# Strassen's seven products for the first FFN product, with the sums of w1's quarters kept in DRAM

## The chip, the cores and the metric

The kernel runs on one core of one Trainium2 chip. Times are device microseconds of one execution. Before the change the median of three runs is 784.04 us (782.01 to 784.25).

## The reference

Four batches of 768 tokens pass through attention with 8 heads of 64 channels (4 sink keys and a window of 128), then a Fourier mix, and then an FFN with a normalization in front:

```python
X = np.fft.fft(np.fft.fft(x, axis=1), axis=2)
u = x + np.real(X).astype(np.float32)
mu = np.mean(u, axis=-1, keepdims=True)
var = np.mean((u - mu) ** 2, axis=-1, keepdims=True)
un = (u - mu) / np.sqrt(var + 1e-06)
ch = np.maximum(un @ w_ch1, 0.0) @ w_ch2
return (u + ch).astype(np.float32)
```

`w_ch1` is 512 x 2048 and `w_ch2` is 2048 x 512. Their entries come as 64-bit floats.

## The kernel before, in words

The work has two stages. The first (to about 225 us of the span) is attention and the Fourier mix, one batch after another. The second is the FFN. Only the second is touched.

The 24 blocks of 128 tokens are cut into **groups** of 4, 2, 4, 4, 4, 4 and 2 blocks (L262). The 2048 hidden features are cut into 16 **feature blocks** f of 128. For one group and one f:

- `ch1` (L612) makes the first product: the weights are w1's block f, the moving operand is the normalized tokens, turned so that channels lie on partitions. Each operand is split into a high and a low part, and a product is high x high, high x low and low x high. So there are 4 channel chunks x 3 = 12 matmuls (L620), of 512 columns for a group of four blocks and of 256 for a group of two, into one PSUM bank.
- `relu` (L1119, ScalarE) makes the high part h of the ReLU, and `relu_lo` (L1124, VectorE) the low part.
- `ch2` (L1126) makes the second product: the weights are now h (128 tokens each), the moving operand is w2's block f of 512 columns; 3 matmuls per token block (L1131), accumulated over all f in one bank per token block.

After the last f, `finish` adds the residual (L1135, VectorE) and stores the block (L1136, SyncE's queue).

**Order.** In group 0 the Tile scheduler orders the work. While this group runs, all 32 weight blocks are loaded in turn (`load_w`, L577; w1's and w2's alternate) and converted (`convert`, L585): three VectorE passes (L591 to L593) make a 32-bit float of a 64-bit one, ScalarE takes the high part (L608), GpSimd the low part (L609). What is left of the last batch's Fourier mix runs beside it. All split weights then stay in SBUF. `prepare(1)` normalizes group 1.

Groups 1 to 6 stand under `tc.manual_schedule()` (L1244): each engine runs its instructions in the order in which the code issues them. For each f the code issues `ch1(f)`, the two ReLU steps, and then `advance`, which issues `ch2` of the f before. A product is thus always one block of twelve matmuls ahead of the use of its ReLU. Behind that come three steps of `prepare` for the next group: statistics, normalization (L539), the turn of a block by VectorE's 32 x 32 transposes (L1155), and the split of the turned block (L549 on ScalarE, L554 on VectorE).

PSUM has eight banks: four for the second product's sums, two ("h") for `ch1`, and one each of "fft" and "n", which serve the Fourier mix and the turns.

```python
def advance(item):
    nonlocal prev
    if prev is not None:
        g, f, h, po = prev
        ch2(f, h, po)
        if f == NF - 1:
            finish(g, po, state[g][0])
    prev = item
```

Of the kernel before, what the change touches and what calls it, by code (L numbers as in the profile page):

```python
# [13 lines left out]
I32 = mybir.dt.int32  # L14
# [32 lines left out]
W_FOLD = 12  # L47
NWA, PER_F, PREP = 14, 2, 11
# [3 lines left out]
CONV_AT, CH1_AT = (3, 5, 7, 9), (9, 10)  # L52
# [3 lines left out]
PREP_AT, PREP_M = 1, 3  # L56
RELOAD_AT = 1
# [149 lines left out]
def kernel(  # L207
# [28 lines left out]


# [24 lines left out]
    sizes = [4, 2, 4, 4, 4, 4, 2]  # L262
# [8 lines left out]
    def run(general):  # L271
        tag = "g" if general else ""
        with ExitStack() as p1:
# [302 lines left out]

            def load_w(i):  # L577
                if i < 2 * NF:
                    f, which = divmod(i, 2)
# [5 lines left out]
            def convert(i, pool=None):  # L585

                r = raw.pop(i)
                t = npool.tile([P, 512], I32, tag="qs0", name=f"cv{i}", bufs=QSB)

                w = t if pool is None or i < NWA else ps_fft.tile([P, 512], I32, tag="fft", name=f"cw{i}", bufs=1)  # L590
# [5 lines left out]
                if i < 4:  # L596

                    if i == 0:
                        state["ring"] = npool.tile([P, 8, 512], F32R, tag="ring", name="w_ring", bufs=1)
                    d = [state["ring"][:, 2 * i + j] for j in range(2)]  # L600
                elif W_FOLD <= i < W_FOLD + NHALF:

                    if i == W_FOLD:
                        state["fold"] = [npool.tile([P, NHALF, DM], F32R, tag=t, name=f"w_{t}", bufs=1) for t in ("gh", "gl")]
                    d = [t[:, i - W_FOLD] for t in state["fold"]]
                else:
                    d = [pool.tile([P, 512], F32R, name=f"w{i}_{j}") for j in range(2)]
                A.copy(d[0], tf)  # L608
                G.tensor_tensor(d[1], tf, f32(d[0]), op=ALU.subtract)  # L609
                Wt[divmod(i, 2)] = d  # L610

            def ch1(g, f, unT):  # L612
# [4 lines left out]
                for cc in range(NCC):  # L617
                    cs = slice(P * cc, P * cc + P)
                    for a, x in ((w[0], unT[0]), (w[0], unT[1]), (w[1], unT[0])):
                        T.matmul(ps[:, :tb], a[:, cs], x[:, :, cc, :], start=n == 0, stop=n == 3 * NCC - 1)  # L620
# [3 lines left out]
            def start_ffn(s):  # L624
# [4 lines left out]
                for i in range(4):  # L629
                    at(s + CONV_AT[i], "V", lambda i=i: convert(i))  # L630
# [477 lines left out]
            def relu(g, f, ps):  # L1108
                tb = P * len(groups[g])
                if g == 0 and un_last:  # L1110

                    t = un_last[0][:, 1].rearrange("p i c t -> p (i c t)")
                    h = [t[:, 1024 * (f % 2) + 512 * i:1024 * (f % 2) + 512 * i + 512] for i in range(2)]
                elif g == 0:
                    h = [g0.tile([P, tb], F32R, tag=f"h{i}", name=f"h{i}_{g}_{f}", bufs=2) for i in range(2)]
                else:
                    h = npool.tile([P, 2, tb], F32R, tag="ld", name=f"h_{g}_{f}", bufs=LDB)
                    h = [h[:, 0], h[:, 1]]
                A.activation(h[0], ps[:, :tb], AF.Relu)  # L1119
                return h  # L1120

            def relu_lo(g, ps, h):
                tb = P * len(groups[g])
                V.scalar_tensor_tensor(h[1], ps[:, :tb], 0.0, f32(h[0]), op0=ALU.max, op1=ALU.subtract)  # L1124
# [8 lines left out]
            def finish(g, po, us):  # L1133
                for i, (b, blk) in enumerate(groups[g]):
                    V.tensor_tensor(us[i], po[i], us[i], op=ALU.add)  # L1135
                    nc.sync.dma_start(out[b, blk], us[i])  # L1136
# [14 lines left out]
            def turn_blocks(un, unf, a):  # L1151

                r = slice(32 * a, 32 * a + 32)
                for q in range(4):
                    V.transpose(unf[32 * q:32 * q + 32, :, r],  # L1155
                                un[r].rearrange("p (c q j) -> p c q j", c=NCC, q=4)[:, :, q])

            def prepare(g):

                us = [u_of(b, blk) for b, blk in groups[g]]  # L1160
                slot = un_slots if g % 2 == 0 else un_last[0]
                unT = [slot[:, :len(us) // 2, i] for i in range(2)]
                state[g] = us, unT
# [7 lines left out]
                for i, u in enumerate(us):  # L1171
# [3 lines left out]
                    if g <= 2:  # L1175

                        pool, tag = banks[1 if g == 1 else i % 2][:2]
                        un_turn(b, blk, pool.tile([P, 512], F32, tag=tag, name=f"unt_{g}_{i}", bufs=1))
                        yield
                    else:  # L1180
                        unf = npool.tile([P, NCC, P], F32, tag="qs0", name=f"unf_{g}_{i}", bufs=QSB)
                        un = un_.pop((b, blk))
                        for a in range(4):
                            turn_blocks(un, unf, a)
                            yield
                        un_[b, blk] = unf.rearrange("p c t -> p (c t)")
                    un_hi(b, blk, unT, i)
                    un_lo(b, blk, unT, i)
                    yield


            pw = None
            un_last = []
            with (tc.manual_schedule() if MAN0 else ExitStack()):
                def do(n):
                    nonlocal s
                    for _ in range(n):
                        for e in ENGINES:
                            run_ev(s, e)
                        s += 1  # L1200

                us = [uview(b)[blk] for b, blk in groups[0]]
                po = [ps_o.tile([P, DM], F32, tag=f"o{i}", name=f"o{i}_0") for i in range(len(us))]
                hs = {}
                for f in range(NF):
                    ps = hp.pop(0) if f < 2 else ch1(0, f, unT0)
                    if f == PREP:
                        ch2(f - 1, hs.pop(f - 1), po)
                        pg.close()
                        wl = p1.enter_context(tc.tile_pool(name="wl" + tag, bufs=1))  # L1210
                        un_last.append(wl.tile([P, 2, 2, NCC, 2 * P], F32R, name="un_last"))
                    hs[f] = relu(0, f, ps)
                    relu_lo(0, ps, hs[f])
                    if pw is None:
                        do(PER_F)
                    if f > 0 and f != PREP:
                        ch2(f - 1, hs.pop(f - 1), po)
                    for i in range(2 * f + 4, min(2 * f + 6, 2 * NF)):
                        if i >= NWA and pw is None:
                            while ev:  # L1220
                                do(1)
                            pf.close()
                            pw = p1.enter_context(tc.tile_pool(name="wb" + tag, bufs=1))
                        convert(i, wa if pw is None else pw)
                    if f == PREP:
                        steps = prepare(1)
                    for _ in range(PREP_N if f >= PREP else 0):
                        next(steps, None)
# [115 lines left out]
```

## Time and profile before

| what | value |
|---|---|
| median of three runs | 784.04 us |
| profiled execution, first to last instruction | 781.4 us |
| median less that span | 2.6 us |
| mean granted TensorE clock | 0.996 |
| matmuls of the first FFN product, L620, largest two groups | 576 and 432 |
| matmuls of the second FFN product, L1131, largest group | 876 |
| mean DMA rate over the span | 74 GB/s |

The span is all that the profile shows of an execution; the 2.6 us lie around it. In the rows below, PE is TensorE's matmuls, PEld its weight loads, DVE VectorE, ACT ScalarE, POOL GpSimd, and SPq the DMA queue of SyncE. A row of the timeline has the start and the length in us, the engine, the line, the operation, output <- input, the shape and the count of merged instructions; in brackets stands how long the engine was idle before and what released it. The length of several merged matmuls runs to the modelled end of the last, which overlaps the next ones, so that the pace is read from starts. A row of groups has, behind the bar, the busy time in us and the mean of one in ns, and behind the next bar the idle time before them.

### The profile page before, as it was taken

The numbers are of one execution on the slowest core, as the hardware profiler recorded it, in microseconds if no ns is written. First come the engines' busy times: TensorE is split into PE (matmuls) and PEld (weight loads), VectorE is DVE, ScalarE is ACT, GpSimd is POOL, SyncE is SP. The second block draws the span as 40 slices with busy tenths as digits, with TensorE's granted clock in tenths as the row PEclk, the third lists the DMA queues.
The fourth block names the chain that finished last, engine by engine and source line by source line (L and its number), as shares of the span: only waits on it lengthen the run. The fifth ranks groups of instructions, "written<-read, shape, count | busy, mean of one in ns | idle before, by whom it ended". The sixth has DMA issues, their size and how long they took to land.

```text
span 781.4 us, 11894 instructions
## 1 busy us (share of the span) xinstructions
PE 755.7 (97%) x4379; PEld 617.1 (79%) x4379; DVE 452.4 (58%) x1318; ACT 237.4 (30%) x704; POOL 183.2 (23%) x295
## 2 busy tenths in 40 slices
PE   8999999989998999999999999999999999999996
PEld 6676876867777878899888888888888888888895
DVE  6878587998999589561456424661456424611211
ACT  4787766766533133221111101111111111110110
POOL 2567477577664245100000000000000000000000
PEclk9999999999999999999999999999999999999999
DMA  9763535434214266110100002000200001000100
GB/s 307 250 176 106 146 83 185 120 118 142 84 54 162 96 206 211 56 55 1 55 0 1 1 37 71 1 0 1 81 0 1 1 8 47 1 0 1 55 1 31
DMA packets 41810, 57.67 MB, mean 74 GB/s; under 512 B 2796, under 2 KB 27500, under 8 KB 41360
## 3 DMA queue, kind: packets, MB, share of 16 engines
q1 hardware_dynamic: 41456, 53.07, 21.7%
q0 software_dynamic: 288, 3.76, 1.2%
q8 instruction: 36, 0.59, 0.3%
q14 instruction: 30, 0.25, 0.1%
HBM read 47.37 MB, written 9.45 MB: 73 GB/s over the span
## 4 chain that ended last, share of the span: by engine, by line
PE 81%; DVE 10%; POOL 4%; issue 2%; ACT 2%; DMA 0%; SPq 0%; ACTq 0%; DVEq 0%; POOLq 0%
PE o L1131 33%; PE h L620 33%; PE xt L798 4%; PE s L703 3%; PE pt L760 2%; DVE cv L592 1%; PE za L395 1%; DVE sm L722 1%; DVE cv L593 1%; ACT sm L728 1%; PE zb L395 1%; ACT pta L767 1%; DVE cv L591 1%; DVE s L709 1%; PE warm L877 1%
## 5 line engine op out<-in xcount | busy, mean ns | idle before, releaser
L1131 PE MATMUL o<-w,h 128*128 128x512 f32 x876 | 217.2, 395 | 0.0
L1124 DVE SCALAR_TENSOR_TENSOR h<-h,h 128x512 fp32r<-128x512 f32 (+1 forms) x107 | 65.4, 612 | 249.1 <-ACT h L1119 248.9
L1131 PEld LDWEIGHTS o<-w,h 128*128 128x128 f32 x876 | 163.4, 189 | 35.6
L1119 ACT ACTIVATE h<-h 128x512 fp32r<-128x512 f32 (+1 forms) x107 | 57.2, 535 | 367.2 <-PE h L620 361.0
L620 PE MATMUL h<-un_slots,w 128*128 128x512 f32 (+1 forms) x576 | 124.7, 365 | 0.0
L620 PEld LDWEIGHTS h<-un_slots,w 128*128 128x128 f32 x576 | 99.6, 188 | 19.6
L620 PE MATMUL h<-un_last,w 128*128 128x512 f32 (+1 forms) x432 | 89.0, 355 | 0.0
L620 PEld LDWEIGHTS h<-un_last,w 128*128 128x128 f32 x432 | 72.7, 188 | 12.8
L728 ACT ACTIVATE sm<-sm,mx 128x132 f32<-128x132 f32 x192 | 76.0, 400 | 4.7 <-DVE mx L722 4.6
L1155 DVE STREAM_TRANSPOSE unf<-un 32x128 f32<-32x128 f32 x224 | 67.7, 302 | 3.2
L703 PE MATMUL s<-ring,q 64*128 64x260 f32 x320 | 49.2, 412 | 6.6 <-DVE mx L722 3.0
L722 DVE CUSTOM_DVE_ANT_0 sm<-s,mask 128x132 f32<-128x132 f32 x192 | 48.5, 293 | 8.2 <-PE s L701 3.1
L703 PEld LDWEIGHTS s<-ring,q 64*128 64x128 f32 x320 | 26.8, 185 | 19.2 <-issue 4.5
L609 POOL TENSOR_TENSOR w<-cv,w 128x512 fp32r<-128x512 f32 x25 | 33.8, 1353 | 30.3 <-ACT w L608 30.3
L798 PE MATMUL xt<-ptl,ldv 128*64 128x128 f32 x384 | 39.3, 285 | 0.2 <-POOL ptl L776 0.2
L728 ACT ACTIVATION_READ_ACCUMULATOR sm<-sm,mx 128x1 f32 x192 | 36.8, 192 | 0.0
L767 ACT COPY pta<-pt 128x512 f32<-128x512 f32 x48 | 28.1, 585 | 27.0 <-PE pt L760 26.6
L1131 PE MATMUL o<-w_ring,h 128*128 128x512 f32 x144 | 35.6, 392 | 0.0
L709 DVE COPY_PREDICATED s<-older,s 128x256 f32<-128x256 uint8 x80 | 33.7, 421 | 1.6 <-PE s L703 1.6
L776 POOL TENSOR_SCALAR_AFFINE_SELECT ptl<-pta 128x512 f32<-128x512 f32 x48 | 32.6, 679 | 8.1 <-ACT pta L767 8.1
L798 PEld LDWEIGHTS xt<-ptl,ldv 128*64 128x64 f32 x384 | 21.9, 136 | 15.1 <-issue 4.7
L798 PE MATMUL xt<-pta,ldv 128*64 128x128 f32 x320 | 31.7, 274 | 0.3 <-POOL pta L784 0.3
(197 smaller groups left out, 1040.6 us busy)
## 6 DMA issues: line engine op xcount, KB each, us to landing
raw<-in_moe_w_ch_dram SPq DMA_DIRECT2D x32, 512.0 KB, 4.2
ldv<-in_v_dram SPq DMA_DIRECT2D x28, 256.0 KB, 3.4
ring<-in_qk_dram SPq DMA_DIRECT2D x24, 264.0 KB, 4.7
out_dram<-u SPq DMA_DIRECT2D x24, 256.0 KB, 2.1
q<-in_qk_dram SPq DMA_DIRECT2D x20, 256.0 KB, 4.2
cst<-in_dft_dram POOLq DMA_DIRECT2D x1, 3348.0 KB, 12.8
ud<-us SPq DMA_DIRECT2D x12, 256.0 KB, 2.2
u<-ud SPq DMA_DIRECT2D x2, 1024.0 KB, 5.1
```

Of the source, the lines that this page charges most:

```text
L609: G.tensor_tensor(d[1], tf, f32(d[0]), op=ALU.subtract)
L620: T.matmul(ps[:, :tb], a[:, cs], x[:, :, cc, :], start=n == 0, stop=n == 3 * NCC - 1)
L703: T.matmul(ps[:, j, :P + W], st["q", g][rows, hp, :], keys(g, 2 * hp + j), start=True, stop=True)
L709: V.copy_predicated(ps[:, :, P + NS:P + W], older[qi > 2], ps[:, :, 0:P])
L722: V.tensor_tensor_reduce(sm[:, h % 4], ps[:, j, P:P + W], mask[min(qi, 3)], -SCALE, 3.0e38, ALU.add, ALU.min, accum_out=mx[:, 0, h:h + 1])
L728: A.activation(sm[:, h % 4], sm[:, h % 4], AF.Exp, bias=mx[:, 0, h:h + 1], scale=-1.0, accum_out=mx[:, 1, h:h + 1])
L767: A.copy(a, st.pop(("pt", g, hp // 2)))
L798: T.matmul(ps[D * j:D * j + D, p, :], st["v", kb(g) - i][:, h, :], a[:, h % 4, :], start=i == 0, stop=i == n - 1)
L1119: A.activation(h[0], ps[:, :tb], AF.Relu)
L1124: V.scalar_tensor_tensor(h[1], ps[:, :tb], 0.0, f32(h[0]), op0=ALU.max, op1=ALU.subtract)
L1131: T.matmul(po[i], a[:, ts_], x, start=f == 0 and n == 0, stop=f == NF - 1 and n == 2)
L1155: V.transpose(unf[32 * q:32 * q + 32, :, r], un[r].rearrange("p (c q j) -> p c q j", c=NCC, q=4)[:, :, q])
```

## The change

The groups are now six of four blocks. Group 0 computes as before. For groups 1 to 5 the first product is made by Strassen's scheme in Winograd's form, with seven products instead of eight. The tokens of a group are halved (256 each), the 512 channels are halved, and two feature blocks (2p, 2p + 1) are paired: a 2 x 2 by 2 x 2 block product.

- **w1's sums.** In group 0, when a pair of w1's blocks is converted, `combine_w1` makes the four sums of its quarters on GpSimd (four passes of 128 x 256), splits them (ScalarE and GpSimd, two passes each of 128 x 512) and stores them to DRAM; the three quarters that are used as they are, are stored too. `w_dram` holds seven split operands per pair. w1 is no longer kept in SBUF; its place is a ring of two pairs.
- **The tokens' sums.** A group's turned blocks lie in `xf`. `sums(g)` makes four sums on GpSimd, and `put(k)` splits operand k (ScalarE, GpSimd) right after product k of the last iteration of the group before has been issued.
- **The loop.** An iteration covers four feature blocks (two pairs); a group has 4. Each of its seven products is 12 matmuls of 256 columns: 2 pairs x 2 channel chunks x 3. The operands come from DRAM into nine places of 512 KB, two DMAs per product, issued nine products ahead. The products use three banks in the order A B C A B C B, accumulating, and VectorE's sums between them turn them into the four quarters of the result: C11, C22, C12, C21.
- **ReLU and the second product.** `halves` splits a quarter's ReLU (ScalarE, VectorE) and puts it in the list `units`. `unit()` takes the next of that list and issues its 12 matmuls of 512 columns. It is called after products 1, 3, 4 and 6.
- w1's blocks and w2's are now converted in pairs (`W_ORDER`), and from the third block on the scratch of a conversion lies in the "fft" bank.

The core of the diff:

```diff
-    sizes = [4, 2, 4, 4, 4, 4, 2]
+    sizes = [4] * 6
+            def combine_w1(p, pool):
+                t = state.pop(("t", p))
+                b11, b21, b12, b22 = t[:, 0, :256], t[:, 0, 256:], t[:, 1, :256], t[:, 1, 256:]
...
+                G.tensor_tensor(q[:, 1], b12, b11, op=ALU.subtract)
+                G.tensor_tensor(q[:, 0], b22, q[:, 1], op=ALU.subtract)
+                G.tensor_tensor(q[:, 2], b22, b12, op=ALU.subtract)
+                G.tensor_tensor(q[:, 3], b21, q[:, 0], op=ALU.subtract)
+                for j in (0, 2):
+                    A.copy(o[:, j:j + 2, 0], q[:, j:j + 2])
+                    G.tensor_tensor(o[:, j:j + 2, 1], q[:, j:j + 2], f32(o[:, j:j + 2, 0]), op=ALU.subtract)
+                nc.sync.dma_start(w_dram[p][:, 3:7], f32(o).rearrange("p k s c -> p k (s c)"))
...
+            def split(h, x):
+                A.activation(h[0], x, AF.Relu)
+                V.scalar_tensor_tensor(h[1], x, 0.0, f32(h[0]), op0=ALU.max, op1=ALU.subtract)
...
+            W_PLACE = (0, 3, 4, 1, 5, 2, 6)
+            BANK = "ABCABCB"
...
+                def start():
+                    G.tensor_tensor(new(2), a21, a22, op=ALU.add)
+                    G.tensor_tensor(new(1), sm[2], a11, op=ALU.subtract)
+                    G.tensor_tensor(new(4), a11, a21, op=ALU.subtract)
+                def put(k):
+                    if k == 5:
+                        G.tensor_tensor(new(5), a12, sm[1], op=ALU.subtract)
+                    x = {0: a11, 3: a12, 6: a22}.get(k)
+                    x = sm[k] if x is None else x
+                    hi, lo = (t[:, k].rearrange("p (c t) -> p c t", c=2) for t in state["x"])
+                    A.copy(hi, x)
+                    G.tensor_tensor(lo, x, f32(hi), op=ALU.subtract)
...
+                def product(n, ps):
...
+                    for j in range(2):
+                        for c in range(2):
+                            cs, xs = slice(P * c, P * c + P), slice(256 * c, 256 * c + 256)
+                            for m, (a, x) in enumerate(((0, xh), (0, xl), (1, xh))):
+                                T.matmul(ps[:, 256 * j:256 * j + 256], w[:, j, a, cs], x[:, xs],
...
+                    load(n + NWS)
...
+                def halves(g, it, odd, half, x):
+                    h = hring[:, len(units) % 4]
+                    units.append((g, it, odd, half, h))
+                    split([h[:, j].rearrange("p j t -> p (j t)") for j in range(2)], x)
+                done = [0]
+                def unit():
+                    if done[0] == len(units):
+                        return
+                    g, it, odd, half, h = units[done[0]]
+                    done[0] += 1
...
+                for n in range(NWS):
+                    load(n)
...
+                        for k in range(7):
...
+                            product(n, ps[BANK[k]])
+                            n += 1
+                            a, b, c = (ps.get(x) for x in "ABC")
+                            put(k)
+                            if k == 0:
+                                A.copy(p1c, a)
+                            elif k == 1:
+                                V.tensor_tensor(u2, b, p1c, op=ALU.add)
+                                unit()
+                                step()
+                            elif k == 3:
+                                halves(g, it, 0, 0, a)
+                                unit()
+                                step()
+                                if it == 0:
+                                    reload(g - 1)
+                            elif k == 4:
+                                V.tensor_tensor(u3, b, p1c, op=ALU.add)
+                                V.tensor_tensor(c22, u3, c, op=ALU.add)
+                                halves(g, it, 1, 1, c22)
+                                unit()
+                                step()
+                            elif k == 5:
+                                V.tensor_tensor(c12, u2, c, op=ALU.add)
+                                halves(g, it, 1, 0, c12)
+                            elif k == 6:
+                                V.tensor_tensor(c21, b, p1c, op=ALU.add)
+                                halves(g, it, 0, 1, c21)
+                                unit()
+                            step()
```

`put` does something only in the last iteration of a group (`it == NIT - 1`), after the remaining steps of `prepare` and `start()`.

More of the change, by code (lines that the diff above doesn't have):

```diff
@@ L55 @@
 PREP_N = 3
-PREP_AT, PREP_M = 1, 3
-RELOAD_AT = 1
+NPR, NIT, NWS = NF // 2, NF // 4, 9
 QSB = 3
@@ L235 @@
     x0_dram = dpool.tile([B * H, D], F32, name="x0d")
+    w_dram = [dpool.tile([P, 7, 512], F32, name=f"wd{i}") for i in range(NPR)]
     prm = cpool.tile([P, 2, 2], I32, name="prm")
@@ L595, in convert @@
                 tf = t.bitcast(F32)
[L596 to L603, printed above, removed]
+                if which == 0:
+                    if f == 0:
+                        state["ring"] = npool.tile([P, 2, 4, 2, 256], F32R, tag="ring", name="w_ring", bufs=1)
+                    fb = state["ring"][:, f // 2 % 2]
+                    d = [fb[:, 0:2, j] if f % 2 == 0 else fb[:, 3:1:-1, j] for j in range(2)]
+                    tf = tf.rearrange("p (h c) -> p h c", h=2)
+                    A.copy(d[0], tf)
+                    G.tensor_tensor(d[1], tf, f32(d[0]), op=ALU.subtract)
+                    Wt[f, 0] = [[d[j][:, cc // 2, P * (cc % 2):P * (cc % 2) + P] for cc in range(NCC)] for j in range(2)]
+                    if f % 2 == 1:
+                        nc.sync.dma_start(w_dram[f // 2][:, 0:3], f32(fb[:, 0:3]).rearrange("p k s c -> p k (s c)"))
+                        state["t", f // 2] = state["tw"].bitcast(F32)
+                    return
@@ L1149, in reload @@
                     nc.sync.dma_start(U[b][:, l[0]:l[-1] + 1, :], u_dram[b + 1][:, l[0]:l[-1] + 1, :])
[L1151 to L1156, printed above, removed]
+            W_PLACE = (0, 3, 4, 1, 5, 2, 6)
+            BANK = "ABCABCB"
             def prepare(g):
                 us = [u_of(b, blk) for b, blk in groups[g]]
-                slot = un_slots if g % 2 == 0 else un_last[0]
-                unT = [slot[:, :len(us) // 2, i] for i in range(2)]
-                state[g] = us, unT
+                xf = state["xf"]
                 for i, u in enumerate(us):
@@ L1179, in prepare @@
                         yield
                     else:
-                        unf = npool.tile([P, NCC, P], F32, tag="qs0", name=f"unf_{g}_{i}", bufs=QSB)
                         un = un_.pop((b, blk))
                         for a in range(4):
-                            turn_blocks(un, unf, a)
+                            r = slice(32 * a, 32 * a + 32)
+                            for q in range(4):
+                                V.transpose(place[32 * q:32 * q + 32, :, r],
+                                            un[r].rearrange("p (c q j) -> p c q j", c=NCC, q=4)[:, :, q])
@@ L1185, in prepare @@
                             yield
[L1186 to L1189, printed above, removed]
-            pw = None
[L1193 to L1228, printed above, removed]
-                for _ in steps:
-                    pass
-                ch2(NF - 1, hs.pop(NF - 1), po)
-                finish(0, po, us)
```

189 lines of the change are left out of this document (131 added, 58 removed).

## The prediction

> **What bounds the kernel now.** I read the page first (busy shares, slices, chain), then the waits of TensorE after 205 us, then the timeline of single stages, and last the groups by form and the stretches.
>
> ```profile
> span 781.4 us, 11894 instructions
> PE 755.7 (97%) x4379; PEld 617.1 (79%) x4379; DVE 452.4 (58%) x1318; ACT 237.4 (30%) x704; POOL 183.2 (23%) x295
> ...
> PE o L1131 33%; PE h L620 33%; PE xt L798 4%; PE s L703 3%; PE pt L760 2%; DVE cv L592 1%; PE za L395 1%; DVE sm L722 1%; DVE cv L593 1%; ACT sm L728 1%; PE zb L395 1%; ACT pta L767 1%; DVE cv L591 1%; DVE s L709 1%; PE warm L877 1%
> ...
> L1131 PEld LDWEIGHTS o<-w,h 128*128 128x128 f32 x876 | 163.4, 189 | 35.6
> ```
>
> TensorE is busy 97% of the span, and two thirds of the chain are the matmuls of the two FFN products (L620, L1131). The stage that the change rewrites is groups 1 to 6:
>
> ```profile
> 322.92 5.64 PE L1131 MATMUL o<-w,un_last 128*128 128x512 f32 x24
> ...
> 326.57 2.73 DVE L1135 TENSOR_TENSOR u<-o,u 128x512 f32<-128x512 f32 x4 [2.06 <-PE o L1131]
> 327.29 2.37 SPq L1136 DMA_DIRECT2D out_dram<-u  x4
> 328.41 2.99 PE L620 MATMUL h<-un_last,w_ring 128*128 128x256 f32 x24
> ...
> 771.89 2.95 PE L1131 MATMUL o<-w,h 128*128 128x512 f32 x12
> ```
>
> It runs from 328.41 to 774.84 (771.89 + 2.95), 446.4 us, with no idle TensorE time that the waits name. The price of a matmul is read from starts, since the ends overlap:
>
> ```profile
> 762.10 1.54 PE L620 MATMUL h<-un_slots,w 128*128 128x256 f32 x12
> ...
> 763.48 1.55 PE L1131 MATMUL o<-w,h 128*128 128x512 f32 x6
> 763.68 0.39 ACT L1119 ACTIVATE h<-h 128x256 fp32r<-128x256 f32 x1 [2.40 <-PE h L620]
> 764.10 0.42 DVE L1124 SCALAR_TENSOR_TENSOR h<-h,h 128x256 fp32r<-128x256 f32 x1 [2.36 <-ACT h L1119]
> ```
> ```profile
> 280.28 2.96 PE L620 MATMUL h<-un_slots,w 128*128 128x512 f32 x12
> 283.07 2.96 PE L1131 MATMUL o<-w,h 128*128 128x512 f32 x12
> 285.87 2.96 PE L620 MATMUL h<-un_slots,w 128*128 128x512 f32 x12
> ```
>
> Twelve of 256 columns take 1.38 us, 0.115 each; 24 of 512 take 5.59 us, 0.233 each. So a 256-column matmul costs half of a 512-column one, its weight load hidden, and cutting the columns into 256 loses nothing.
>
> **The change, part by part.** *Fewer matmuls.* Five groups of four blocks now run 4 iterations each. An iteration has seven products of 12 matmuls of 256 columns, 84 x 0.115 = 9.66 us, and four units of the second product, 48 x 0.2329 = 11.18 us: 20.84 us, and 416.8 for 20 iterations, against 446.4. That is **-29.6 us**, if TensorE never waits.
>
> *New waits.* Here it does. In code order its queue reads: product 3, unit C11, product 4, unit C22, products 5 and 6, unit C12, the next iteration's products 0 and 1, unit C21, product 2. `units` is a queue, but it is empty when product 3 ends (the call after product 1 took the only entry), so C11 and C22 are taken in the call right after they are put in. Before, `advance` put the next block's twelve matmuls between a ReLU and its use. Nothing reorders this region, which is under the manual schedule:
>
> ```profile
> 504.48 1.26 DVE L1155 STREAM_TRANSPOSE unf<-un 32x128 f32<-32x128 f32 x4
> ...
> 505.78 0.62 ACT L549 CAST un_slots<-unf 128x512 fp32r<-128x512 f32 x1 [2.05 <-DVE unf L1155]
> 506.43 0.69 DVE L554 TENSOR_TENSOR un_slots<-unf,un_slots 128x512 fp32r<-128x512 f32 x1 [0.69 <-ACT un_slots L549]
> 507.04 0.54 DVE L539 TENSOR_SCALAR un<-u,stat 128x512 f32<-128x512 f32 x1
> ```
>
> VectorE sits idle 0.69 us for ScalarE while the next block's normalization (L539), which needs nothing of that, is next in the code: neither planner nor hardware moved it up. I expect the same of TensorE. The links of the waits:
>
> ```profile
> 224.65 0.62 ACT L365 CAST gh<-f 128x512 fp32r<-128x512 f32 x1 [1.17 <-DVE f L359]
> ...
> 225.32 0.61 PE L395 MATMUL za<-cst,gh 128*128 128x386 f32 x2 [0.47 <-ACT gh L365]
> ...
> 276.23 0.69 DVE L592 SCALAR_TENSOR_TENSOR cw<-raw,cw 128x512 int32<-128x512 int32 x1
> ...
> 277.03 0.69 DVE L593 SCALAR_TENSOR_TENSOR cv<-raw,cw 128x512 int32<-128x512 int32 x1
> ...
> 508.65 0.60 ACT L1119 ACTIVATE h<-h 128x512 fp32r<-128x512 f32 x1 [2.25 <-PE h L620]
> ```
>
> A reader starts 0.20 us after TensorE has gone on (763.48 to 763.68); VectorE follows ScalarE by 0.03; a dependent VectorE operation follows its forerunner by 0.80; a ReLU takes 0.60, a VectorE pass 0.69; TensorE starts 0.05 after ScalarE ends (225.27 to 225.32). What waits is the load of h as weights (189 ns), which then lies bare. With T the end of the product:
> - C11: 0.20 + 0.60 + 0.05 + 0.19 = 1.04. The third matmul needs the low half: VectorE runs 0.83 to 1.52, so it starts at 1.76 instead of 1.04 + 0.47; 0.25 more. **1.29**.
> - C22: two VectorE sums first, 0.20 + 0.80 + 0.69 = 1.69, then 0.03 + 0.60 + 0.05 + 0.19, so 2.56, and 0.25: **2.81**.
> - C12: sum to 0.89, ReLU to 1.52, first matmul at 1.76; product 6 covers 1.38. 0.38 + 0.25 = **0.63**.
> - C21: about 2.3 us of chain under unit C12 and two products, 5.5 us: nothing.
>
> VectorE is free when each chain starts: two steps of transposes (1.26 each) follow the low half of C11 and end before unit C11 and product 4 do. Sum 4.73 per iteration, **+94.6 us** in all. From below, 4.16 (83 us) if the weight load hides; from above, 5.2 (104 us) if each of the waits loses another 0.15.
>
> *The clock.* The longest wait is long enough to matter:
>
> ```profile
> 253.67 1.66 PE L422 MATMUL a<-cst,za 128*128 128x258 f32 x6 [2.52 <-DVE zb L410]
> ```
> ```profile
> 250.02:253.43 3.41, 1.13 (x9) 0.88 (x7) 3.38 (x6) 1.25 (x3) 1.38 (x1) 1.00 0.57 204
> 253.43:256.84 3.41, 3.17 (x11) 2.90 (x12) 0.88 (x2) 1.48 (x4) 1.28 (x1) 0.50 0.50 159
> ...
> 103.24:106.66 3.42, 2.29 (x20) 2.12 (x19) 1.46 (x7) 2.43 (x7) 2.85 (x6) 1.00 0.85 224
> ```
>
> The columns after the length are PE, PEld, DVE, ACT and POOL; the granted clock stands before the DMA share. A wait of 2.52 us made 3.41 us with 2.28 idle, and the next 3.41 us were granted half the clock; a stretch with 1.13 idle was followed by no loss. If the stretches lie at a fixed pitch, and the limit is midway at 1.7 us, the 2.56 us of C22 trips it in (3.41 - 2.56 + 2 x 0.86) / 3.41 = 75% of the iterations, and each costs about 1.5 us of matmul time: 22 us. Ends: 0 and 30 (every iteration). I take **+22**. The Trainium skill (TensorE: Matmul & The Clock Gate, "HAM oscillation") gives the rule that idle gaps above about 3.4 us re-throttle; by it no gap here would, and the sum would be 22 us lower. This trace's 2.52 us gap contradicts it.
>
> *Last iteration of a group.* `put` places a high-half copy (0.62) ahead of the ReLU of C11, and GpSimd runs while VectorE does the low half of C22 from SBUF:
>
> ```profile
> L609 POOL TENSOR_TENSOR w<-cv,w 128x512 fp32r<-128x512 f32 x25 | 33.8, 1353 | 30.3 <-ACT w L608 30.3
> ...
> L593 DVE SCALAR_TENSOR_TENSOR cv<-raw,cv 128x512 int32<-128x512 int32 x12 | 13.5, 1124 | 0.1
> ...
> L593 DVE SCALAR_TENSOR_TENSOR cv<-raw,cw 128x512 int32<-128x512 int32 x18 | 12.4, 686 | 1.7
> ```
>
> Both inputs in SBUF cost 1124 ns beside a working GpSimd, against 686 with one in PSUM. Up to 1.1 + 0.62 us, four times: **+7**; 0 if GpSimd pauses there. GpSimd's own eleven passes, 14.9 us, fit in 25 us.
>
> *Group 0 and the hand-over.* Per feature block GpSimd does two splits (2.7 us) and half of `combine_w1`:
>
> ```profile
> L460 POOL TENSOR_TENSOR us<-us,d 128x255 f32<-128x255 f32 x3 | 2.2, 732 | 10.7 <-DVE d L448 10.7
> ```
> ```profile
> 285.00:295.00 10.00, 10.00 (x45) 8.08 (x44) 9.31 (x15) 3.31 (x6) 4.97 (x5) 1.00 0.64 206
> ```
>
> (4 x 0.73 + 2 x 1.35) / 2 = 2.8, so 5.5 of TensorE's 5.59 us; VectorE is at 9.31 of 10 already. It just fits, but then the 14.9 us of `sums` come at the end, and `load(0)` stands in SP's queue behind four stores that wait for the adds (to 329.30), with some 4 us to land:
>
> ```profile
> GB/s 307 250 176 106 146 83 185 120 118 142 84 54 162 96 206 211 56 55 1 55 0 1 1 37 71 1 0 1 81 0 1 1 8 47 1 0 1 55 1 31
> ...
> raw<-in_moe_w_ch_dram SPq DMA_DIRECT2D x32, 512.0 KB, 4.2
> ```
>
> The first product then starts near 333.5 instead of 328.41, 5 us late; with a GpSimd remainder I take **+10**, between 0 and 30 (20.5 us of queue in the open, and the w1 sums' stores ahead of raw loads in SP's queue). A gain is not excluded, as 12 passes of 1124 ns become 686, but VectorE is not what ends this stage. The stream itself is 14 x 256 KB, 3.67 MB per 25 us, 147 GB/s beside the 307 reached in the first slice, nine products ahead: free. Uncovered, 512 KB at 307 would be 1.7 us per product, 0.3 over its matmuls.
>
> Sum against the profiled 781.4: -29.6 + 94.6 + 22 + 7 + 10 = +104. The span lies 2.6 us under the median 784.04; the forecast is **888**.
>
> **Rivals.**
> - *The waits are covered* (the order isn't kept, so that product 4 runs under C11's chain and the change gains what it counts): 784 - 30 + 10 + 2 = 766. For it: the matmul count is certain. Against: the idle VectorE above. It decides if fewer than 1.5 of the 4.73 us stay per iteration. 0.08; another 0.01 for an even result.
> - *Waits, but no half clock*: 888 - 22 = 866, if the limit lies above 2.56 us of idle. The trace's one case speaks against. 0.22. The Trainium skill's rule, above, is the page that would have it so.
> - *GpSimd bounds group 0*: all 20.5 us of its queue in the open, and TensorE waits for splits queued behind sums: 20 us more, 908. For it: 5.5 of 5.59. Against: combined sums are needed only later, so the planner can put them behind. 0.13.
>
> **How the numbers follow.** The forecast has 0.56. Its own range is 860 to 915, by the ends of the waits (-12, +9), the clock (-22, +8) and group 0 (-10, +20), not all at once. The no-clock case with short waits reaches 852, the GpSimd case with long ones 928. Below 850 are the 0.09 of the covered case and little else. Range 850 to 928. A difference of 0.3% (2.4 us) is about what a measurement of this kernel tells from none: faster 0.08, same 0.01, slower 0.91.
>
> **What would show it.** Right: TensorE idle before L1131's counterpart in two places of each iteration, about 1.0 us released by ScalarE and 2.6 by the same after two VectorE sums; an iteration of 25 to 27 us; a granted clock of 0.5 in many stretches after 335 us; 84 matmuls of 256 columns at 0.115. Wrong: the unit's matmuls following their product without a gap, an iteration near 21 us, waits released by a DMA, or group 0 ending much after 335.

## The result, and the profile after

The changed kernel takes **910.25 us** (median of four runs, 908.42 to 912.4), against 783.6 for the kernel before in the same runs (782.01 to 784.25). The ratio is **1.161**, with a 95% interval of 1.1575 to 1.1644. The profiled execution took 912.4 us, its span is 910.7, and the mean granted clock fell from 0.996 to 0.951.

The head of the profile's page, the slices of GpSimd, of the clock and of the DMA rate, and the costliest group:

```profile
span 910.7 us, 13834 instructions
...
PE 795.4 (87%) x4899; PEld 644.8 (71%) x4899; DVE 518.8 (57%) x1400; ACT 268.8 (30%) x743; POOL 289.8 (32%) x398
...
POOL 2574684765556897001310013100230003300000
...
PEclk9999999999989899999999999999989999999999
...
GB/s 310 251 94 180 59 183 148 120 94 44 160 159 297 267 299 258 330 117 137 141 229 150 128 118 118 252 139 147 129 113 168 162 139 129 123 173 131 162 1 50
...
L1330 PE MATMUL o<-w,hring 128*128 128x512 f32 x780 | 231.0, 438 | 53.9 <-ACT hring L1140 46.3
```

TensorE went from 97% busy to 87%. The last row is the largest group of the second product's matmuls: TensorE stood idle 53.9 us ahead of them, 46.3 of it until a ReLU's high part (`hring`, L1140) was there. GpSimd is at 5 to 9 tenths through group 0 (slices 11 to 16), and the DMA rate there is up to 299 GB/s; it is 330 in slice 17, where the loop begins, and 110 to 250 behind it, around the estimate of 147.

The waits of TensorE from 356 us on, with the sum, the count and the longest in us:

```profile
PE o L1330 <- ACT hring L1140: 61.4, 40, 2.5
PE o L1330 <- DVE hring L1141: 6.3, 9, 0.9
PE pC L1302 <- DMA w_a<-wd: 1.7, 1, 1.7
```

Forty waits for ScalarE's half of a ReLU are as many as two in each of the 20 iterations. The DMA stream made TensorE wait 1.7 us here, and 0.5 once more, both at the loop's start.

Where the 129.3 us between the spans (910.7 - 781.4) lie is read from the timeline, at the loop's first product and at its last unit:

```profile
355.39 1.58 PE L1302 MATMUL pA<-x,w_a 128*128 128x256 f32 x12
...
882.57 1.57 PE L1302 MATMUL pA<-x,w_a 128*128 128x256 f32 x12
884.24 0.60 ACT L1140 ACTIVATE hring<-pA 128x512 fp32r<-128x512 f32 x1 [6.40 <-PE pA L1302]
884.87 0.69 DVE L1141 SCALAR_TENSOR_TENSOR hring<-pA,hring 128x512 fp32r<-128x512 f32 x1 [5.50 <-ACT hring L1140]
884.89 3.29 PE L1330 MATMUL o<-w,hring 128*128 128x512 f32 x12 [0.75 <-ACT hring L1140]
888.02 1.58 PE L1302 MATMUL pB<-x,w_a 128*128 128x256 f32 x12
889.63 0.69 DVE L1374 TENSOR_TENSOR tmp<-pB,tmp 128x512 f32<-128x512 f32 x1 [4.07 <-PE pB L1302]
890.36 0.69 DVE L1375 TENSOR_TENSOR tmp<-tmp,pC 128x512 f32<-128x512 f32 x1
891.13 0.63 ACT L1140 ACTIVATE hring<-tmp 128x512 fp32r<-128x512 f32 x1 [6.30 <-DVE tmp L1375]
...
891.82 3.29 PE L1330 MATMUL o<-w,hring 128*128 128x512 f32 x12 [2.23 <-ACT hring L1140]
894.94 1.58 PE L1302 MATMUL pC<-x,w_a 128*128 128x256 f32 x12
896.35 1.57 PE L1302 MATMUL pB<-x,w_b 128*128 128x256 f32 x12
...
898.02 6.05 PE L1330 MATMUL o<-w,hring 128*128 128x512 f32 x24
```

The loop runs from 355.39 to 904.07 (898.02 + 6.05): 548.7 us, 102.3 more than the 446.4 of groups 1 to 6 before. It begins at 355.39 instead of 328.41: 27.0 more. The two make the 129.3.

The rows are one iteration of the last group, where no next group is prepared. Product 3 (882.57) hands over at 882.57 + 1.41, the pace of its neighbours (894.94 to 896.35). Its ReLU starts 0.26 us later, and unit C11 starts at 884.89, after 0.91 us of nothing; it then lasts 3.13 us to the next product instead of 2.79, since its third matmul waits for the low part: 1.25 us lost. Product 4 (888.02) hands over at 889.43; two VectorE sums, the ReLU, and unit C22 at 891.82: 2.39 us bare and 0.33 in the unit, 2.72 lost. Product 6 covers most of C12's chain: 896.35 + 1.41 to 898.02 are 0.26 bare, and about 0.3 in the unit.

### The profile page after: what moved, and what is told of

It is laid out like the page before. It is cut to its first block, busy times and chain, and to the rows that moved or that the text cites. A ratio compares the mean times of both kernels' runs of the same rounds, so it can differ in the third digit from the quotient of the medians.

```text
span 910.7 us, 13834 instructions
## 1 busy us (share of the span) xinstructions
PE 795.4 (87%) x4899; PEld 644.8 (71%) x4899; DVE 518.8 (57%) x1400; ACT 268.8 (30%) x743; POOL 289.8 (32%) x398
## 4 chain that ended last, share of the span: by engine, by line
PE 64%; DVE 16%; POOL 7%; ACT 6%; issue 4%; DMA 1%; SPq 1%; ACTq 0%; POOLq 0%; DVEq 0%
PE o L1330 30%; PE pC L1302 6%; PE pB L1302 6%; PE pA L1302 6%; ACT hring L1140 4%; PE xt L828 3%; PE s L733 3%; PE o L1148 2%; PE pt L790 2%; DVE tmp L1374 2%; DVE tmp L1375 2%; DVE tmp L1380 1%; DVE hring L1141 1%; PE h L650 1%; DVE sm L752 1%
## 5 line engine op out<-in xcount | busy, mean ns | idle before, releaser
L1330 PE MATMUL o<-w,hring 128*128 128x512 f32 x780 | 231.0, 438 | 53.9 <-ACT hring L1140 46.3
L1330 PEld LDWEIGHTS o<-w,hring 128*128 128x128 f32 x780 | 153.0, 207 | 111.3 <-ACT hring L1140 56.7
L1140 ACT ACTIVATE hring<-tmp 128x512 fp32r<-128x512 f32 x60 | 37.9, 631 | 246.3 <-DVE tmp L1380 109.3
L1200 DVE STREAM_TRANSPOSE xf<-un 32x128 f32<-32x128 f32 x256 | 77.3, 302 | 3.4
L1141 DVE SCALAR_TENSOR_TENSOR hring<-tmp,hring 128x512 fp32r<-128x512 f32 x60 | 48.0, 800 | 45.5 <-ACT hring L1140 45.5
L1330 PE MATMUL o<-w_gh,hring 128*128 128x512 f32 x120 | 48.4, 444 | 15.6 <-ACT hring L1140 15.1
L650 PE MATMUL h<-un_slots,w_ring 128*128 128x512 f32 x192 | 52.0, 414 | 8.2 <-POOL w_ring L611 4.7
L1302 PE MATMUL pB<-x,w_b 128*128 128x256 f32 x408 | 53.1, 279 | 0.0
L1302 PEld LDWEIGHTS pB<-x,w_b 128*128 128x128 f32 x408 | 50.8, 188 | 1.0
L1148 PE MATMUL o<-w,h 128*128 128x512 f32 x156 | 44.3, 434 | 6.6 <-ACT w L624 3.3
L1226 POOL TENSOR_TENSOR x<-s,x 128x512 fp32r<-128x512 f32 x20 | 25.6, 1284 | 58.9 <-ACT x L1225 58.7
L1330 PEld LDWEIGHTS o<-w_gh,hring 128*128 128x128 f32 x120 | 23.5, 199 | 29.1 <-ACT hring L1140 18.7
L1148 PEld LDWEIGHTS o<-w,h 128*128 128x128 f32 x156 | 32.5, 211 | 15.7 <-POOL w L625 4.1
```

What stands on the lines that cost most here:

```text
L650: T.matmul(ps[:, :tb], a[cc], x[:, :, cc, :], start=n == 0, stop=n == 3 * NCC - 1)
L1140: A.activation(h[0], x, AF.Relu)
L1141: V.scalar_tensor_tensor(h[1], x, 0.0, f32(h[0]), op0=ALU.max, op1=ALU.subtract)
L1148: T.matmul(po[i], a[:, ts_], x, start=f == 0 and n == 0, stop=f == NF - 1 and n == 2)
L1200: V.transpose(place[32 * q:32 * q + 32, :, r], un[r].rearrange("p (c q j) -> p c q j", c=NCC, q=4)[:, :, q])
L1302: T.matmul(ps[:, 256 * j:256 * j + 256], w[:, j, a, cs], x[:, xs], start=BANK.index(BANK[k]) == k and j == c == m == 0, stop=j == c == 1 a ...
```

## The experiments

The theory: in the loop, TensorE waits for what it has itself just made, because `units` is empty whenever an entry is put in; the long waits halve the clock behind them; and group 0 ends late because GpSimd, with w1's sums and splits, no longer keeps up. The rivals: the stream from DRAM delays the loop; a VectorE conversion in the one "fft" bank, the SyncE queue or DMA contention delays group 0.

### One unit of lag

`unit()` leaves the newest entry in the list and takes the one before it; the list is emptied behind the last iteration. No product, sum or unit is left out.

```diff
-                def unit():
+                def unit(drain=False):
...
-                    if done[0] == len(units):
+                    if len(units) - done[0] < (1 if drain else 2):
                         return
...
-                    unit()
+                    unit(True)
```

> A unit of the second product is issued only when a second one is waiting behind it, so each ReLU has at least one product of cover; nothing else changes. Theory (TensorE's queue waits for the quarter just made, 4.7 us per iteration, and the waits bring the half clock): the waits and the half clock both go from the loop, which falls from 548.7 to about 425 us, and the kernel to 780 to 795 us. Rival (the operands streamed from DRAM set the pace of the loop, the waits only show it): an iteration needs as long as before, the waits move to the products, with a DMA as releaser, and the time stays above 870.

Measured: 779.59 us (776.16 to 783.15), just under the range expected, ratio 0.9953 (0.9928 to 0.9979), span 774.4. TensorE's timeline of one iteration and of the next one's start, and the loop's two ends:

```profile
351.83 1.52 PE L1302 MATMUL pA<-x,w_a 128*128 128x256 f32 x12
...
452.32 1.58 PE L1302 MATMUL pA<-x,w_b 128*128 128x256 f32 x12
...
473.20 1.52 PE L1302 MATMUL pA<-x,w_b 128*128 128x256 f32 x12
...
759.38 8.40 PE L1330 MATMUL o<-w,hring 128*128 128x512 f32 x36
```

And all the waits of its TensorE from 356 us on:

```profile
PE pC L1302 <- DMA w_a<-wd: 1.6, 1, 1.6
PE pB L1302 <- issue: 0.4, 1, 0.4
```

No unit (L1330) is among the waits, and the rows have no bracket, so that no idle time stands ahead of them; an iteration is 473.20 - 452.32 = 20.88 us. The forecast's bare count of matmuls was 20.84. The loop is 767.78 - 351.83 = 415.9 us, against the forecast's 416.8. The same DMAs, sums and splits run as in the changed kernel, so that its loss in the loop was the order of the units; the DMA rival falls. No stretch of the loop has half the clock. What is left of the loss is the start: 351.83, 23.4 us later than before, and the 30.5 us of the loop less those 23.4 are the 7.0 by which the spans differ.

A repeat with more runs:

> The kernel with the lag of one unit once more, with more rounds, to settle whether it is faster than the kernel before: the loop is 20 iterations of 20.8 us as in its first run, and only group 0, whose order the scheduler fixes but whose waits and half clocks fall differently from run to run, moves the time. If the first run's 0.995 holds, 776 to 783; if it was a lucky draw like those of its variants, 781 to 786 and no difference from the kernel before.

780.5 us (777.34 to 783.97, twelve runs), ratio **0.9966** (0.9949 to 0.9982): faster than the kernel before, but by 0.3% only. Its loop started at 355.91, 4.1 us later than in the first profile of the same kernel, so that a loop start read from one profile is good to some 4 us.

### The clock alone

Sixteen matmuls of 256 columns, whose result nobody reads, fill the wait of C22 and end before its unit can start. They are written behind `halves` of C22:

```diff
                                 halves(g, it, 1, 1, c22)
+                                wp, wt = banks[(it + 1) % 2][:2]
+                                wm = wp.tile([P, 512], F32, tag=wt, name=f"wm_{g}_{it}", bufs=1)
+                                for _ in range(16):
+                                    T.matmul(wm[:, :256], Wt[0, 1][0][:, :P], Wt[0, 1][0][:, :256], start=True, stop=True)
                                 unit()
```

> Sixteen matmuls of 256 columns without use are put between product 4 and unit C22, so that TensorE is busy for some 1.8 of the 2.4 us that it waits there; the wait itself keeps its length. Theory (the idle stretch brings half a clock about once per iteration): no stretch of half clock is left in the loop, and the time falls by 20 to 35 us, to 875 to 890. Rival (the half clock comes from something else, or costs nothing because it lies in other waits): 905 to 915.

Measured: 887.61 us (883.31 to 889.5), ratio 1.1297 (1.1257 to 1.1337): 22.6 us less than the changed kernel. TensorE's timeline at the filling, and ScalarE's copy of product 0 (L1362) in three of five iterations running:

```profile
473.49 1.58 PE L1302 MATMUL pB<-x,w_b 128*128 128x256 f32 x12
474.91 2.08 PE L1380 MATMUL wm<-w 128*128 128x256 f32 x16
477.30 3.29 PE L1330 MATMUL o<-w,hring 128*128 128x512 f32 x12 [0.30 <-ACT hring L1140]
```
```profile
462.89 0.59 ACT L1362 COPY tmp<-pA 128x512 f32<-128x512 f32 x1 [2.76 <-PE pA L1302]
488.34 0.59 ACT L1362 COPY tmp<-pA 128x512 f32<-128x512 f32 x1 [2.38 <-PE pA L1302]
...
567.66 0.59 ACT L1362 COPY tmp<-pA 128x512 f32<-128x512 f32 x1 [2.80 <-PE pA L1302]
```

Unit C22 still starts 477.30 - 474.91 = 2.39 us after its product has handed over: the same wait as in the changed kernel, now filled. The iteration is 488.34 - 462.89 = 25.45 us (by the forecast's terms 20.84 + 4.73 = 25.57), where the changed kernel's takes about 27.2. One half-clock stretch is left in the loop, near its start. The loop takes 526.3 us (354.56 to 880.90), 22.3 less than 548.7. So the difference of 22.6 us in the median is the clock's price in the loop by itself, and the forecast's term was 22. The four iterations to 567.66, the end of a group among them, took 567.66 - 462.89 = 104.77 us, 2.8 more than 4 x 25.5.

### Unit C11 behind product 4

A smaller cure, made on the changed kernel: the units are taken in the same order, but C11's call is moved behind product 4, where C22's chain begins.

```diff
                             elif k == 3:
                                 halves(g, it, 0, 0, a)
-                                unit()
...
                                 halves(g, it, 1, 1, c22)
                                 unit()
+                                unit()
```

> On the changed kernel: unit C11 is moved from behind product 3 to behind product 4, ahead of unit C22; nothing else changes. Theory (each wait is the chain of its ReLU less what stands between): C11 has product 4 as cover, C22 has unit C11 (2.8 us of cover for 2.56), and the wait of C12 stays, 0.6 us; an iteration of 21.4 us and 785 to 797 in all. Rival (the lag of a whole unit is needed, since the half clock stays as long as any wait is left): above 805.

Measured: 832.27 us (832.09 to 833.76), ratio 1.062 (1.0595 to 1.0645). The expectation missed by 35 us. The timeline behind the start of unit C11 (505.79):

```profile
505.93 2.50 DVE L1200 STREAM_TRANSPOSE xf<-un 32x128 f32<-32x128 f32 x8
508.45 0.69 DVE L1373 TENSOR_TENSOR tmp<-pB,tmp 128x512 f32<-128x512 f32 x1
...
510.64 3.31 PE L1330 MATMUL o<-w,hring 128*128 128x512 f32 x12 [1.93 <-ACT hring L1140]
```

C11's wait is gone: product 4 covers it. But C22's first sum (L1373) starts at 508.45 and not when product 4 is done, near 506: two steps of transposes (2.50 us) stand ahead of it in VectorE's queue, and unit C22 (510.64) is left waiting 1.93 us; eleven waits of this kind make 18.0 us of the loop. In the changed kernel unit C11 and product 4 gave VectorE 4.2 us for them; here product 4 alone does. Iterations with transposes take 25.2 to 25.5 us, those with other steps 22.0 to 23.0, and those of the last group, which has no steps, 21.34 to 21.5, against 21.4 as expected. The mechanism on TensorE was right, and the queue beside it was not looked at. Half the clock is granted in four stretches of the loop instead of eighteen. So the time is above the rival's 805, but not for the rival's reason, a half clock that stays.

### Group 0: GpSimd's sums left out

On the changed kernel, `combine_w1` stores bytes that are there already in place of the sums, so that the four GpSimd sums and the four passes of splitting (two on GpSimd, two on ScalarE) are left out and the traffic stays:

```diff
-                G.tensor_tensor(q[:, 1], b12, b11, op=ALU.subtract)
...
-                nc.sync.dma_start(w_dram[p][:, 3:7], f32(o).rearrange("p k s c -> p k (s c)"))
+                fb = state["ring"][:, p % 2]
+                nc.sync.dma_start(w_dram[p][:, 3:7], f32(fb).rearrange("p k s c -> p k (s c)"))
```

> The sums of w1's quarters and their splits (GpSimd and ScalarE) are left out; the same number of bytes is stored from the ring of w1's blocks instead, so that the products use wrong operands of the same size. Theory (GpSimd's queue is what starves group 0): the loop starts 10 to 25 us earlier and the time falls by as much, to 885 to 900. Rival (the scratch of the conversions in the fft bank, or the pairwise order, is what delays group 0): 905 to 915.

Measured: 897.73 us (897.28 to 900.12), ratio 1.1452 (1.1426 to 1.1478), 12.5 less than the changed kernel. TensorE's timeline at the loop's start:

```profile
338.32 1.58 PE L1293 MATMUL pA<-x,w_a 128*128 128x256 f32 x12
...
343.03 2.37 PE L1293 MATMUL pB<-x,w_a 128*128 128x256 f32 x10 [3.14 <-DMA w_a<-wd]
```

The loop starts at 338.32, 17.1 us earlier than 355.39, and then gives back 3.14 at its second product, whose operands have not landed. Of the 27.0 us of group 0, then, some 17 hang on these passes, and some 10 stay without them. The same 40 us of the span, by stretch, with the columns PE, PEld, DVE, ACT, POOL, clock, DMA share and GB/s, for the kernel before, the changed one and the one without sums:

```profile
295.00:335.00 40.00, 40.00 (x197) 33.36 (x196) 29.12 (x49) 10.77 (x20) 12.71 (x10) 1.00 0.41 139
```
```profile
295.00:335.00 40.00, 35.58 (x146) 27.86 (x147) 31.04 (x45) 18.14 (x32) 34.83 (x33) 0.91 0.83 284
```
```profile
295.00:335.00 40.00, 39.33 (x176) 31.48 (x175) 31.13 (x46) 16.25 (x28) 24.67 (x20) 1.00 0.85 307
```

GpSimd works 34.83 of the 40 us in the changed kernel against 24.67 without the sums, and TensorE has 4.4 us of gaps and 9% less clock; without them it is nearly full. VectorE's 31 us are the same in both, and so is the DMA share.

### Group 0: the rivals

The scratch of the conversions in SBUF for the first fourteen blocks instead of the "fft" bank (on the changed kernel):

```diff
-                w = t if pool is None else ps_fft.tile([P, 512], I32, tag="fft", name=f"cw{i}", bufs=1)
+                w = t if i < 14 else ps_fft.tile([P, 512], I32, tag="fft", name=f"cw{i}", bufs=1)
```

> The scratch of the first 14 conversions lies in SBUF, as it did before the change, and the fft bank is left to the Fourier mix for so long. Theory (GpSimd starves group 0): within 5 us of 910. Rival (the bank is what delays group 0): the loop starts 10 us or more earlier, and the time is 900 or less.

910.01 us (906.01 to 913.74), ratio 1.1583 (1.155 to 1.1616), loop start 356.78: no change. The bank isn't it.

Stores of w1's operands cut to one of seven, and all products loading that one (on the kernel with one unit of lag, like all that follow):

```diff
-                        nc.sync.dma_start(w_dram[f // 2][:, 0:3], f32(fb[:, 0:3]).rearrange("p k s c -> p k (s c)"))
+                        nc.sync.dma_start(w_dram[f // 2][:, 0:1], f32(fb[:, 0:1]).rearrange("p k s c -> p k (s c)"))
...
-                nc.sync.dma_start(w_dram[p][:, 3:7], f32(o).rearrange("p k s c -> p k (s c)"))
```

> On the kernel with the lag of one unit. Of a pair's seven stored operands only the first is stored (256 KB instead of 1.75 MB per pair), and every product loads that one; GpSimd's sums run as before, without use. Theory (GpSimd's queue is what starves group 0): within 4 us of the 779.6 of the lagged kernel. Rival (the stores take the DMA engines or SP's queue from the raw loads, about 300 GB/s in this stage): the loop starts 8 us or more earlier, and the time is 772 or less.

784.78 us (783.19 to 788.65), ratio 1.0014 (1.0001 to 1.0028), 5.2 above the kernel with lag: outside the theory's 4 us, and the wrong way for the rival. Its stretch of the same 40 us:

```profile
295.00:335.00 40.00, 35.70 (x146) 27.60 (x145) 30.36 (x45) 16.51 (x29) 33.38 (x33) 0.91 0.56 184
```

Against the changed kernel's stretch the DMA rate fell from 284 to 184 GB/s, while TensorE's 35.7 us, its clock of 0.91 and GpSimd's 33 us stayed; the loop started at 362.76, later and not earlier. The stores and their traffic are not what holds group 0; why the start came later is not shown.

### Group 0: relieving GpSimd in part

Five edits on the kernel with lag tried to keep the sums and take the pressure off. `combine_w1` issued one feature block later:

```diff
-            combine_w1(0, g0)
...
-                if f % 2 == 1 and f // 2 + 1 < NPR:
-                    combine_w1(f // 2 + 1, g0)
+                if f % 2 == 0:
+                    combine_w1(f // 2, g0)
```

> On the kernel with the lag of one unit. The sums of a pair of w1's blocks are issued one feature block later in the code, behind the conversions of the next pair, so that the scheduler may let the splits that TensorE waits for go first on GpSimd. Theory (TensorE waits in group 0 for splits that stand behind sums in GpSimd's queue): 3 to 10 us less than 779.6. Rival (GpSimd has too much to do in total, whatever the order): within 3 us.

Group 1's token sums and their splits on VectorE instead of GpSimd (the other passes of `sums` likewise):

```diff
+                E = V if n == 1 else G
...
-                    G.tensor_tensor(new(2), a21, a22, op=ALU.add)
+                    E.tensor_tensor(new(2), a21, a22, op=ALU.add)
```

> On the kernel with the lag of one unit. The eleven passes of the sums and splits of group 1's tokens run on VectorE (0.69 us each) instead of GpSimd (1.3); those of the later groups stay. Theory (at the end of group 0 GpSimd is the last to finish, with VectorE mostly idle): the loop starts 3 to 8 us earlier, 772 to 777. Rival (the hand-over waits for the operands' loads behind the stores in SP's queue): within 2 us of 779.6.

Both of these:

> Both of the last two edits. If they act on different waits, the gains add: 766 to 775. If both only relieve the same queue, the gain is that of the larger one.

One of the two low-part splits of `combine_w1` on VectorE:

```diff
-                    G.tensor_tensor(o[:, j:j + 2, 1], q[:, j:j + 2], f32(o[:, j:j + 2, 0]), op=ALU.subtract)
+                    (V if j else G).tensor_tensor(o[:, j:j + 2, 1], q[:, j:j + 2], f32(o[:, j:j + 2, 0]), op=ALU.subtract)
```

> On the kernel with the lag of one unit: one of the two low-part splits of w1's sums per pair runs on VectorE (0.69 us) instead of GpSimd (1.3). GpSimd has then 9.5 us of work per pair of feature blocks, VectorE some 10.6, TensorE 11.2. Theory (the total of GpSimd's work starves group 0): the loop starts 3 to 8 us earlier, 772 to 778. Rival (VectorE, slowed beside GpSimd, is as near to the limit): within 2 us of 779.6 to 783.

And both of them, with `V.tensor_tensor` in that line:

> As before, with both low-part splits on VectorE: GpSimd 8.2 us per pair, VectorE 11.3, TensorE 11.2. Theory: about as share_one, with VectorE now the later one: 772 to 782. Rival (VectorE bounds group 0 at once): 785 or more.

| kernel | us | ratio | 95% interval | loop start, us |
|---|---|---|---|---|
| lag, five runs | 779.59 | 0.9953 | 0.9928 to 0.9979 | 351.83 |
| lag, again | 780.5 | 0.9966 | 0.9949 to 0.9982 | 355.91 |
| sums later | 782.9 | 0.9997 | 0.9976 to 1.0018 | 352.84 |
| token sums on VectorE | 784.87 | 1.0018 | 0.9996 to 1.004 | 356.29 |
| both of these | 781.24 | 0.9979 | 0.9958 to 1.0001 | 356.39 |
| one split on VectorE | 782.33 | 0.9982 | 0.9964 to 0.9999 | 362.65 |
| two splits on VectorE | 782.93 | 0.9991 | 0.9971 to 1.0012 | 358.36 |

None gains anything on the lag alone, so that none of the theories' gains came; only the rival of one split on VectorE (779.6 to 783) was met. Issuing the sums one block later doesn't help, and neither does moving GpSimd's passes to VectorE, a few at a time, though leaving w1's sums out did. Where the sums come later, where the token sums are on VectorE and with both, the loop's first product also waits for the DMA of its operands (1.5, 0.7 and 0.8 us), and the loop takes 418.1 to 420.0 us instead of 415.9. **Open:** why nothing helps. Group 0 stands under the scheduler, which lays the whole stage out anew at each of these edits; and leaving the sums out took two passes per pair from ScalarE too, and may have eased VectorE's passes beside GpSimd. The runs don't separate these three. The new order of the conversions (w1's and w2's blocks in pairs) was not tested by itself.

## Why the prediction was right, and where it was not

The forecast was 888 with a range to 928, and the result is 910.25. The direction and the three largest terms came out as worked; two small ones were too small, and one of them, group 0, makes most of the difference. Two bounds in its text don't follow from its own terms (866 - 12 is 854, not 852; 908 + 9 + 8 is 925, not 928), which changes nothing here.

- *Fewer matmuls, -29.6.* Right: with the waits taken away the same loop takes 415.9 us, where 416.8 was forecast.
- *New waits, 4.73 per iteration.* Right, in place and size: 1.25 for C11 (forecast 1.29), 2.72 for C22 (2.81), about 0.6 for C12 (0.63); the iteration with a full clock is 25.45 (25.57). The rival of the covered waits is refuted by the idle times before L1330.
- *The clock, +22.* Right in sum: 22.6 by the filled wait. The parts partly offset each other, which is luck: the forecast was 15 losses of 1.5 us, and there were 18 stretches of half the clock, of which the filled wait gave back 17, at 1.3 each. The assumed limit of about 1.7 us of idle in a stretch of 3.41 is close, but the runs show no sharp one. Two pairs of neighbouring stretches of the changed kernel:

```profile
368.04:371.46 3.42, 1.53 (x13) 1.32 (x11) 1.38 (x2) 0.41 (x1) 0.00 (x0) 1.00 1.05 403
371.46:374.87 3.41, 3.13 (x12) 2.29 (x13) 1.61 (x7) 0.22 (x1) 0.00 (x0) 1.00 1.08 428
...
422.63:426.04 3.41, 1.77 (x7) 1.17 (x8) 2.55 (x7) 0.63 (x1) 0.00 (x0) 1.00 0.42 147
426.04:429.46 3.42, 3.42 (x12) 2.84 (x11) 1.40 (x5) 0.00 (x0) 1.74 (x2) 0.50 0.00 0
```

  A stretch with 3.41 - 1.77 = 1.64 us idle was followed by half the clock, one with 3.42 - 1.53 = 1.89 idle was not. In this profile no stretch with less than 1.6 us idle lost the clock, and every one with 1.98 or more did; between the two, both occur. The Trainium skill (TensorE: Matmul & The Clock Gate, "HAM oscillation") asks for gaps above about 3.4 us; the longest wait in the loop is 2.5 us, so by that rule the loop would have kept its clock. The measurement decides: the rival without half clocks, 866, lacks the 22.6 us.
- *Last iteration of a group, +7.* Right in kind, somewhat short: 2.8 us per group with a full clock, some 11 for four. GpSimd's part shows in the timeline of one such iteration:

```profile
561.43 1.63 DVE L1141 SCALAR_TENSOR_TENSOR hring<-tmp,hring 128x512 fp32r<-128x512 f32 x1 [0.76 <-ACT hring L1140]
...
563.12 3.90 PE L1330 MATMUL o<-w,hring 128*128 128x512 f32 x10 [0.93 <-DVE hring L1141]
```

  The low half of C22 takes 1.63 us beside a GpSimd pass (L1221, 561.23 to 562.51), where it takes 0.69 in the last group, and the unit, begun at 561.45, stops for it after two matmuls, 0.93 us.
- *Group 0 and the hand-over, +10.* This is the term that failed, by its size: the loop starts 27.0 us later, and "group 0 ending much after 335" was one of the forecast's own signs of being wrong. "It just fits" was the step: GpSimd's 5.5 us per feature block were taken to hide beside TensorE's 5.59, and no lost clock was counted for group 0. The stretch from 190 us to the end of group 0, before and after, with the columns as in the stretches above:

```profile
190.00:328.41 138.41, 132.07 (x712) 109.53 (x709) 115.30 (x195) 46.49 (x104) 66.80 (x63) 0.99 0.38 123
```
```profile
190.00:355.39 165.39, 144.69 (x730) 116.29 (x729) 122.24 (x219) 62.80 (x132) 116.05 (x121) 0.93 0.55 196
```

  TensorE's idle time grew from 6.3 us (138.41 - 132.07) to 20.7, by 14.4. Its busy time grew by 12.6 on nearly the same matmuls; most of this is the clock, which fell from 0.99 to 0.93: 23.9 us at half the clock instead of 3.4, some 10 us by an estimate from these two lengths ((23.9 - 3.4) / 2). GpSimd went from 66.80 to 116.05 us busy, but it is not full throughout. TensorE's waits from 190 to 356 us:

```profile
PE h L650 <- POOL w_ring L611: 4.7, 6, 1.5
PE h L650 <- ACT w_ring L610: 3.3, 1, 3.3
PE o L1148 <- ACT w L624: 3.3, 1, 3.3
...
PE o L1148 <- POOL w L625: 2.9, 3, 1.7
```

  The splits of the weights (L610, L611, L624, L625) make TensorE wait 14.2 us in eleven places (4.7 + 3.3 + 3.3 + 2.9; the columns as in the waits above); the row left out is of the Fourier mix. GpSimd ends 7.6 us of these waits. The other 6.6 are two waits for ScalarE's high part, which itself had waited for a conversion on VectorE (L601):

```profile
252.15 0.62 ACT L624 CAST w<-cv 128x512 fp32r<-128x512 f32 x1 [3.47 <-DVE cv L601]
...
296.45 0.62 ACT L610 CAST w_ring<-tw 128x512 fp32r<-128x512 f32 x1 [5.28 <-DVE tw L601]
```

  A wait like the second, of 3.4 us, stands in the kernel without the sums too. The rival "GpSimd bounds group 0", which put the start at 30 us late and the time at 908, had 0.13. Its numbers came nearest, but its mechanism is shown only in part: some 17 us hang on the sums and their splits, and the cause of the other 10 stays open. The forecast's own case, with the remainder hidden, did not come. The other bound of the term, traffic in SyncE's queue and in DRAM, cost nothing that the kernel with few stores would have got back.

The sum with the measured terms: 416.8 (the forecast's count, which the kernel with lag bore out) + 92 (20 x 4.61, the iteration of 25.45 less 20.84) + 22.3 + 11 + 2.2 (the two DMA waits) = 544.3 for the loop, against 548.7, and 27.0 ahead of it; 4.4 us of the loop are not accounted for.

## What to carry to other kernels

When an algorithm saves arithmetic but lengthens the chain from a product to its use, write the queue so that the consumer lags one full unit behind its producer: the same change lost 129 us of span or gained 7 by that one condition. Before moving a consumer, read what stands in the queues of the other engines on its chain, as the unit moved behind product 4 shows. And what a change saves in one stage is worth only what its preparation costs in the stage ahead: 30.5 us gained in the loop were paid with 23.4 ahead of it, and in the changed kernel some 17 of such a loss hung on the added passes.

## What the runs showed of the hardware

- In these runs the clock is lost by the idle time within a stretch of 3.41 us: in the changed kernel's profile never with less than 1.6 us idle, always with 1.98 or more, and between them in some stretches only. The idle time can be less than one wait's length where the wait falls across two stretches. In the loop, eighteen stretches had half the clock, typically 27.31 us apart, eight times 3.413, while an iteration takes about 27.2: a period near a multiple of the stretch would keep the wait on the same place of it.
- A VectorE operation beside a running GpSimd pass can be delayed however small it is, but not every one is. The timeline of the changed kernel:

```profile
247.00 1.22 DVE L529 TENSOR_TENSOR stat<-stat 128x4 f32<-128x4 f32 x1
...
248.25 0.17 DVE L531 SCALAR_TENSOR_TENSOR stat<-stat 128x4 f32<-128x4 f32 x1
...
554.55 0.69 DVE L1141 SCALAR_TENSOR_TENSOR hring<-pA,hring 128x512 fp32r<-128x512 f32 x1 [5.85 <-ACT hring L1140]
```

  The first, on four columns, lay beside two GpSimd passes that ran from 245.65 to 248.19, and took 1.22 us; the second came after them and took 0.17. The third lay beside a GpSimd pass too (L1226, 554.10 to 555.38) and took 0.69, as all twenty of its kind do: one of its inputs, pA, is in PSUM. With tmp in SBUF in that place, the same operation took 1.63 (561.43, above).
